# A decode attention and MLP kernel: the tensor engine's wait at a loop's entry, and the layout of the last weight matrix

## The chip, the core and the metric

The kernel runs on one core of one Trainium2 chip. Its engines are TensorE (PE in the profile, its weight loads PEld), VectorE (DVE), ScalarE (ACT), GpSimd (POOL) and SyncE (SP); SP issues nearly all transfers, and its issuing instructions are shown as SPq. The metric is the device time of one execution in microseconds, and the median of several runs is taken. Shorter is better.

## What is computed

One decode step of a transformer block for a batch of 4 tokens, with a cache of 4096 keys and values for each of 32 heads:

```
h  = x + attention(layernorm(x), k_cache, v_cache, wq) @ wo     # D = 640, 32 heads of 128
h2 = h + mish(layernorm(h) @ w1 + b1) @ w2                      # F = 1728
```

Everything is bf16. The key and the value cache are 134 MB each (4 x 32 x 4096 x 128), so the kernel reads 283 MB of memory and does little arithmetic with each number. F = 1728 is 13 chunks of 128 and one of 64.

## The kernel before, in words

**Units and slots.** The batch and the heads are cut into 16 units of 8 heads of one token (`NU` = 16). A unit's keys are one transfer of 128 x 32768 numbers (8.4 MB), and its values another. There are three slots in SBUF, 64 KB on each partition, and keys and values use them in turn: K of unit u and later V of unit u go to slot 2u mod 3 (K of unit 0 to slot 1, and V of unit 0 to slot 0, once wq has been read from there).

**One unit.** VectorE multiplies the keys in place by the broadcast query, in 8 pieces (L585, `times_q`). TensorE sums the products over the head dimension with an identity as weights, 16 matmuls for each quarter (L597, `sums`, into four PSUM banks). VectorE reduces each bank (L572, `reduce`). Then come the maximum (L634, L643, L652), the bias (L665, L674) and the exponentials on ScalarE (L682). TensorE multiplies the *previous* unit's exponentials with its values (L707, `pv`), in program order right behind the current unit's sums, and then closes the unit before that (L739, L741, L760, L767).

**The order of the transfers.** SP issues them in program order, each with the waits it needs: wq, K0, K1, V0, K2, V1, K3, V2, K4 and so on (L333). V of unit u goes into the slot in which K of unit u was, so it waits for that unit's sums. K of unit u+2 waits for the product with the values that lay in its slot, those of unit u-1. The last unit's values come in four parts. Behind them on SP's queue are `wo` (4 transfers), `w1` (5), and `w2` (5; all at L823, in `load`), which go into slots that the last units leave; then the output (L1048).

**Who sets the waits.** The class `Program` records every operation with what it reads and writes, works out the waits (`plan`), and emits each engine's instructions in the recorded order (`emit`). All engines' instructions are straight-line code except TensorE's. Its units 2 to 13 are a loop of 4 turns with 3 units a turn, in which a wait's target is worked out from the turn (`turn * step + base`). A wait inside the loop is kept for an operation only if the engine has not waited for that event before, in the order of the straight program. So that nothing is missed at the first turn, `plan` collects `pe_entry`: for every source, the latest event from before the loop that any operation in the loop depends on. `emit` has TensorE wait for all of these ahead of the loop (L200). Among the sources are other engines' counters and, for unit 2's `pv`, the counter of slot 2, which stands for the transfer of V1. The loop's own wait for that transfer stands in front of `pv`.

**The end.** After the last unit, the 16 outputs are regrouped (L852, L872, L880) and projected with `wo` (L892); a layernorm follows in which the mean is taken out ahead of `w1` and the variance put in afterwards (L929, L937, L971, L983). `h1_pass` (L956) multiplies 14 chunks of columns of `w1` for each of five blocks of 128 rows, so 70 matmuls of 4 columns. The last chunk has only 64 columns; the PSUM rows that it doesn't write are zeroed by VectorE first (L950). The mish function is seven small operations (L852 to L998). `w2_products` (L1024) then does 70 more matmuls, chunk by chunk as parts of `w2` arrive: first the 64 rows left over, then chunks 0 to 5, 6 to 9, 10 and 11, and 12. A residual, a transposition (L1040), a copy (L1047) and the output transfer end the kernel. Chunk c of the hidden vector is rows 128c to 128c+127 of `w2`, one row of 1,280 bytes on a partition.

Of the kernel before, what the change touches and what calls it, by code (L numbers as in the profile page):

```python
# [21 lines left out]
class Program:  # L22
# [53 lines left out]
    def plan(self):  # L76
        by_key = {o.key: o for o in self.ops if o.key is not None}

        def shifted(o, units):
            return by_key.get((*o.key[:-1], o.key[-1] + units)) if o.key else None  # L80


        known = {e: {} for e in self.ENGINES}
        for o in self.ops:
            k = known[o.eng]
            o.waits = []
            for src, d in o.deps.items():
# [12 lines left out]
        before, rest = [], None  # L100
        in_order = [o for o in self.ops if o.eng == "PE"]
        at = [i for i, o in enumerate(in_order) if self.in_loop(o)]
        assert at == list(range(at[0], at[0] + len(body) * turns))
        for t in range(turns):
            for p, b in enumerate(body):
                o = in_order[at[0] + t * len(body) + p]
                assert o is shifted(b, (t - 2) * self.turn), (o.key, b.key)
        self.pe_before = in_order[: at[0]]
        self.pe_after = in_order[at[0] + len(body) * turns :]
        body_waits = [[d for d in b.waits] for b in body]  # L110
        for b in body:
            for d in b.waits:
                assert d.key is not None and d.key[-1] >= self.first + self.turn, (b.key, d.key)


        loop_units = range(self.first, self.last + 1)
        for o in self.ops:
            for d in o.waits:
                d.signal = True
        for o in self.ops:  # L120
            if o.signal and o.key and o.key[-1] in loop_units:
                for u in range(self.first, self.last + 1):
                    same = by_key.get((*o.key[:-1], u))
# [24 lines left out]

        self.body_waits = []
        for b, waits in zip(body, body_waits):  # L150
            out = []
            for d in waits:
                src = d.sem or d.eng
                e = shifted(d, self.turn)
                step = e.count - d.count
                assert step > 0
                for t in range(turns):
                    f = shifted(d, (t - 2) * self.turn)
                    if f is not None and f.key[-1] >= self.first:
# [50 lines left out]
def kernel(  # L210
# [64 lines left out]
    S_BANK, TR, QQ, OB, OT = [("bank", i) for i in range(4)], *[("bank", i) for i in range(4, 8)]  # L275
# [4 lines left out]
    ident = const([128, 128], BF16, "ident")  # L280
# [205 lines left out]
        "DVE", lambda: nc.vector.tensor_copy(out=j_m[:, :], in_=j_f[:, :]), r=["j_f"], w=["j_m"]  # L486
    )

    def f_chunk(rows, c):
        if c < C2:  # L490
            return rows[:, c * 128 : (c + 1) * 128], 128
        return rows[:, FM:F], FREM


    qT_ps = qq_bank[:, 0 : N * H].rearrange("p (b h) -> p b h", b=N)
# [16 lines left out]

    def b1_turned():
        for c in range(FC):
            cols, fw = f_chunk(b1_row, c)
            ins = nc.tensor.matmul(  # L516
                b_ps[0:fw, c : c + 1], lhsT=cols, rhs=ident[0:1, 0:1], start=True, stop=True
            )
        return ins

    def b1_copy():
        nc.vector.tensor_copy(out=b1T[:, 0:C2], in_=b_ps[:, 0:C2])  # L522
        return nc.vector.tensor_copy(out=b1T[0:FREM, C2:FC], in_=b_ps[0:FREM, C2:FC])
# [323 lines left out]
    def do(eng, emit, r=(), w=()):  # L847

        return P.add(eng, emit, r=r, w=w, after=[last_pv])
# [100 lines left out]
    do("DVE", lambda: nc.vector.memset(h1_ps[FREM:128, FC - 1, :], 0.0), (), [QQ])  # L950
    std, rstd = scratch(N), scratch(N)

    def h1_pass(dc):
        for c in (0, C2, *range(1, C2)):
            lhsT, fw = f_chunk(w1_sb[:, dc, :], c)
            ins = nc.tensor.matmul(  # L956
                h1_ps[0:fw, c, :],
                lhsT=lhsT,
                rhs=h2T[:, dc, :],
                start=(dc == 0 and c == 0),  # L960
                stop=(dc == DC - 1 and c == C2 - 1),
            )
        return ins

# [53 lines left out]

    def w2_products(blocks):
        for c in blocks:  # L1020
            rows = 128 if c < C2 else FREM
            w2 = w2_sb[:, c, :] if c < C2 else w2r_sb
            for dc in range(DC):
                ins = nc.tensor.matmul(  # L1024
                    y2T[:, dc, :],
                    lhsT=w2[:, dc * 128 : (dc + 1) * 128],
                    rhs=act_t[0:rows, c, :],
                    start=(c == C2 and dc == 0),
                    stop=(c == C2 - 1 and dc == DC - 1),
                )  # L1030
        return ins

    for name, blocks in ((C2, [C2]), *((k0, range(k0, k1)) for k0, k1 in zip(W2P, W2P[1:]))):
        do("PE", lambda blocks=blocks: w2_products(blocks), [("w2", name), "act"], [S_BANK[1]])
# [48 lines left out]
```

## Time and profile before

| | |
|---|---|
| time, median of 3 runs | 672.83 us (672.2 to 672.95) |
| the profiled execution's own time | 673.69 us |
| its span in the profile | 671.8 us |
| busy: PE, PEld, DVE, ACT, POOL | 380.5, 174.8, 353.2, 88.0, 1.3 us |
| read from memory | 283.35 MB, 422 GB/s over the span |

The span is the time from the first to the last event of the profile; 1.89 us of the execution lie outside it. A row of the waits names the waiting engine with its output and line, what released it, the total of the waits in us, their number and the longest. A row of a timeline has the start and the duration in us, the engine, the line, the operation, output and inputs with their shapes, the number of instructions merged, and in brackets the idle time before it and what ended it. A row of the chain has start, duration, engine or transfer. A row of a windows table has the stretch, its length, the busy time and number of instructions of PE, PEld, DVE, ACT and POOL, TensorE's granted clock, the busy share of the 16 DMA engines and the GB/s that they moved; a transfer packet counts in the window in which it starts. A row of the groups has busy time in us, mean ns of one, and the idle time before.

### The profile page before, as it was taken

How to read it: one execution, taken by the hardware profiler on the slowest of the kernel's cores; microseconds unless marked ns; L12 is line 12 of the kernel's file. 1: busy time of each engine (PE TensorE's matmuls, PEld its weight loads, DVE VectorE, ACT ScalarE, POOL GpSimd, SP SyncE). 2: the span in 40 equal slices, each digit the busy share in tenths (PEclk: the TensorE clock that was granted, in tenths of full speed). 3: DMA queues.
4: the chain of work that ended last, by engine and by line, in shares of the span. 5: the costliest groups of instructions: out<-in, count | busy, mean ns of one | idle time of the engine just before them, and what ended most of it. 6: DMA issues, size and time to landing. Idle time of an engine off the chain costs nothing.

```text
span 671.8 us, 6600 instructions
## 1 busy us (share of the span) xinstructions
PE 380.5 (57%) x2793; PEld 174.8 (26%) x2793; DVE 353.2 (53%) x314; ACT 88.0 (13%) x314; POOL 1.3 (0%) x10
## 2 busy tenths in 40 slices
PE   0366732887282856738184664818375481837764
PEld 0222310333031322213032321303132230313344
DVE  2078840766381836548182754728184563819501
ACT  0102020020202020110202020020202002020211
POOL 0000000000000000000000000000000000000000
PEclk9999975989596796959688796968879695978965
DMA  9999999799999999999999999999999999999997
GB/s 375 438 437 434 433 435 433 328 376 438 433 434 437 437 437 437 433 437 433 421 425 419 437 437 437 433 437 433 433 437 433 437 437 437 434 430 410 412 416 245
DMA packets 8347, 283.62 MB, mean 422 GB/s; under 512 B 835, under 2 KB 2567, under 8 KB 3208
## 3 DMA queue, kind: packets, MB, share of 16 engines
q1 hardware_dynamic: 8318, 283.35, 98.2%
q8 instruction: 12, 0.20, 0.1%
q14 instruction: 7, 0.06, 0.0%
q10 hardware_dynamic: 10, 0.01, 0.0%
HBM read 283.35 MB, written 0.01 MB: 422 GB/s over the span
## 4 chain that ended last, share of the span: by engine, by line
DMA 39%; DVE 28%; PE 20%; another core or an unknown queue 8%; SPq 3%; issue 1%
DMA slot<-in_A_k_cache_dram 33%; DVE slot L585 23%; PE bank L597 14%; PE bank L707 5%; DMA slot<-in_A_v_cache_dram 4%; DVE s_sb L572 3%; SPq L823 3%; DMA slot<-in_B_w_dram 2%; PE bank L665 0%; DVE mx L652 0%; PE bank L643 0%; DVE otn L767 0%; DVE rl L760 0%; PE bank L741 0%
## 5 line engine op out<-in xcount | busy, mean ns | idle before, releaser
L597 PE MATMUL bank<-slot,ident 128*128 128x512 bf16 x1024 | 273.9, 423 | 250.2 <-DVE slot L585 225.6
L585 DVE TENSOR_TENSOR slot<-slot,qb 128x4096 bf16<-128x4096 bf16 x128 | 288.2, 2284 | 145.4 <-DMA slot<-in_A_k_cache_dram 145.4
L597 PEld LDWEIGHTS bank<-slot,ident 128*128 128x128 bf16 x1024 | 101.5, 107 | 408.4 <-DVE slot L585 258.7
L572 DVE TENSOR_REDUCE s_sb<-bank 128x64 f32<-128x512 f32 x64 | 44.0, 688 | 74.5 <-PE bank L597 74.5
L682 ACT ACTIVATE e<-s_sb,nb 128x256 bf16<-128x256 f32 x128 | 63.1, 494 | 46.6 <-DVE nb L674 46.6
L707 PE MATMUL bank<-slot,e 128*32 128x512 bf16 x1024 | 60.7, 391 | 1.5 <-DMA slot<-in_A_v_cache_dram 1.5
L552 ACT CAST qb<-bank 128x128 bf16<-128x128 f32 x16 | 4.2, 265 | 294.5 <-PE bank L543 294.5
L727 ACT COPY o_sb<-bank 128x512 f32<-128x512 f32 x16 | 9.4, 585 | 200.2 <-PE bank L707 200.2
L707 PEld LDWEIGHTS bank<-slot,e 128*32 128x32 bf16 x1024 | 26.5, 99 | 34.1 <-issue 9.0
L652 DVE TENSOR_REDUCE mx<-bank 1x8 f32<-1x128 f32 x16 | 4.5, 279 | 39.9 <-PE bank L643 39.9
L682 ACT ACTIVATION_READ_ACCUMULATOR e<-s_sb,nb 128x1 f32 x128 | 23.9, 187 | 0.0
L741 PE MATMUL bank<-sel,o_sb 128*128 128x8 f32 x128 | 17.4, 263 | 0.0
L741 PEld LDWEIGHTS bank<-sel,o_sb 128*128 128x128 f32 x128 | 16.4, 201 | 0.0
L500 PE MATMUL bank<-xT,slot 128*128 128x4 bf16 x160 | 4.4, 168 | 11.0 <-DMA slot<-in_A_wq_dram 11.0
L665 PE MATMUL bank<-mx,nscale 1*128 1x8 f32 x32 | 6.1, 262 | 5.9 <-DVE mx L652 5.9
L760 DVE RECIPROCAL rl<-bank 128x8 f32<-128x8 f32 x16 | 3.2, 202 | 11.3 <-PE bank L741 11.3
L522 DVE COPY b1T<-bank 128x13 f32<-128x13 f32 x1 | 0.2, 172 | 14.5 <-PE bank L516 14.5
L665 PEld LDWEIGHTS bank<-mx,nscale 1*128 1x128 f32 x32 | 4.7, 183 | 10.6 <-DVE mx L652 10.6
L500 PEld LDWEIGHTS bank<-xT,slot 128*128 128x128 bf16 x160 | 4.3, 104 | 11.1 <-DMA slot<-in_A_wq_dram 11.1
L634 DVE TENSOR_REDUCE pm<-s_sb 128x1 f32<-128x256 f32 x16 | 6.7, 420 | 0.5
L739 PEld LDWEIGHTS bank<-rs,ones_f 128*128 128x128 f32 x32 | 6.1, 198 | 3.2 <-ACT o_sb L727 1.2
L643 PE MATMUL bank<-ident_f,pm 128*1 128x128 f32 x32 | 6.1, 272 | 1.2 <-DVE pm L634 1.2
(73 smaller groups left out, 69.2 us busy)
## 6 DMA issues: line engine op xcount, KB each, us to landing
slot<-in_A_v_cache_dram SPq DMA_DIRECT2D x4, 2048.0 KB, 42.5
slot<-in_A_wq_dram SPq DMA_DIRECT2D x1, 5120.0 KB, 15.5
slot<-in_A_wo_dram SPq DMA_DIRECT2D x4, 1280.0 KB, 33.8
slot<-in_B_w_dram SPq DMA_DIRECT2D x5, 432.0 KB, 29.7
slot<-in_B_w_dram SPq DMA_DIRECT2D x1, 960.0 KB, 20.4
slot<-in_B_w_dram SPq DMA_DIRECT2D x1, 640.0 KB, 19.5
slot<-in_B_w_dram SPq DMA_DIRECT2D x1, 320.0 KB, 10.9
slot<-in_A_k_cache_dram SPq DMA_DIRECT2D x16, 50.2
```

The source lines that it names most:

```text
L500: ins = nc.tensor.matmul(qT_ps[:, :, h], lhsT=wq_sb[:, c, h * Dh : (h + 1) * Dh], rhs=xT[:, c, :], start=(c == 0), stop=(c == DC - 1),)
L572: lambda: nc.vector.tensor_reduce(out=s_sb[:, part * RP : (part + 1) * RP], in_=s_bank[part][:, :].rearrange("p (r w) -> p r w", w=W), axi ...
L585: return nc.vector.tensor_tensor(out=kt, in0=kt, in1=qbs[u % NS][:, k * DQ : (k + 1) * DQ] .unsqueeze(1) .to_broadcast([128, RP, DQ]), op= ...
L597: ins = nc.tensor.matmul(s_bank[part][:, :].rearrange("p (r w) -> p r w", w=W), lhsT=ident[:, :], rhs=kt[:, :, d : d + W], start=(d == 0), ...
L634: lambda: nc.vector.tensor_reduce(out=pm[:, :], in_=s_sb[:, :], axis=AX.X, op=ALU.max),
L643: lambda: nc.tensor.matmul(tr_bank[0:1, 0:128], lhsT=pm[:, :], rhs=ident_f[:, :], start=True, stop=True),
L665: lambda: nc.tensor.matmul(nb_ps, lhsT=nscale[:, :], rhs=mx[:, :], start=True, stop=True),
L682: ins = nc.scalar.activation(out=e2[:, :, h, :], in_=s_sb[:, :].rearrange("p (g r) -> p g r", r=RQ), func=ACT.Exp, bias=nb[:, h : h + 1], ...
L707: ins = nc.tensor.matmul(o_bank[t : t + G * RQ, :], lhsT=e2[:, g, :, :], rhs=vt[:, g * RQ : (g + 1) * RQ, :], start=(g < CT), stop=(g >= N ...
L727: lambda: nc.scalar.copy(out=o_sb[:, :], in_=o_bank[:, :]),
L741: ins = nc.tensor.matmul(o_ps, lhsT=o_sb[:, r * Dh : (r + 1) * Dh], rhs=sel[:, r, :], start=(r == 0), stop=(r == RQ - 1),)
L823: lambda: nc.sync.dma_start(out=out_ap, in_=in_ap),
```

## The change

There are two edits.

The first is one condition in `plan`: an event enters `pe_entry` only if it isn't a transfer's (`d.sem is None`). TensorE's wait for slot 2 at the loop's entry goes; those for DVE, ACT and POOL stay. The wait inside the loop, in front of `pv`, is untouched.

The second changes which hidden column goes with which partition. For the first 12 chunks, chunk 2m takes the even and chunk 2m+1 the odd columns of 256 (`f_rows`), so that one partition holds two neighbouring rows of `w2`, and its transfers move 2,560 contiguous bytes where they moved 1,280. `w1` and `b1` keep their layout in SBUF, and TensorE reads every second column of them as weights. Chunk 12 stays as it was. The last chunk takes the last 128 columns, so that it repeats the last 64 columns of chunk 12 in its upper half; the `w2` rows for these are zeros, written by GpSimd (`w2r`), and the 64 real rows go to partitions 64 to 127. With every chunk 128 wide, three small operations fall away: the zeroing of PSUM (L950) and of `b1T` (L389), and the second of two copies of `b1T` (L523). Both matmul loops now go through the chunks in order.

```diff
-                if d.key is None or d.key[-1] < self.first:
+                if d.sem is None and (d.key is None or d.key[-1] < self.first):
...
+    OVER = 128 - FREM
...
-    P.add("POOL", lambda: nc.gpsimd.memset(b1T[:, :], 0.0), w=["b1T"])
...
+    def f_rows(c):
+        if c < C2 - C2 % 2:
+            f0 = c // 2 * 256 + c % 2
+            return slice(f0, f0 + 255, 2)
+        f0 = c * 128 if c < C2 else F - 128
+        return slice(f0, f0 + 128)
...
-    P.add("DVE", b1_copy, r=[OT], w=["b1T"])
+    P.add("DVE", lambda: nc.vector.tensor_copy(out=b1T[:, :], in_=b_ps), r=[OT], w=["b1T"])
...
-    w2r_sb = wend2[0:FREM, C2 * D : nw2]
-    w2_view = B_w2[0:FM, :].rearrange("(k p) n -> p k n", k=C2)
+    w2r_sb = wend2[:, C2 * D : nw2]
+    C2E = C2 - C2 % 2
+    w2_view = B_w2[0 : C2E * 128, :].rearrange("(m p k) n -> p m (k n)", p=128, k=2)
...
-    load(w2r_sb, B_w2[FM:F, :], i2, C2 * D, nw2, ("w2", C2))
+    P.add("POOL", lambda: nc.gpsimd.memset(w2r_sb, 0.0), w=["w2r"], after=[last_pv])
+    P.add(
+        "SP",
+        lambda: nc.sync.dma_start(out=w2r_sb[OVER:128, :], in_=B_w2[FM:F, :]),
+        w=["w2r"],
+        sem="w2r",
+    )
     for k0, k1 in zip(W2P, W2P[1:]):
-        load(w2_sb[:, k0:k1], w2_view[:, k0:k1], i2, k0 * D, k1 * D, ("w2", k0))
+        if k0 < C2E:
+            to = wend2[:, k0 * D : k1 * D].rearrange("p (m n) -> p m n", n=2 * D)
+            of = w2_view[:, k0 // 2 : k1 // 2]
+        else:
+            to, of = w2_sb[:, k0, :], B_w2[k0 * 128 : k1 * 128, :]
+        load(to, of, i2, k0 * D, k1 * D, ("w2", k0))
...
-    do("DVE", lambda: nc.vector.memset(h1_ps[FREM:128, FC - 1, :], 0.0), (), [QQ])
...
-        for c in (0, C2, *range(1, C2)):
-            lhsT, fw = f_chunk(w1_sb[:, dc, :], c)
+        for c in range(FC):
             ins = nc.tensor.matmul(
-                h1_ps[0:fw, c, :],
-                lhsT=lhsT,
+                h1_ps[:, c, :],
+                lhsT=w1_sb[:, dc, f_rows(c)],
```

More of the change, by code (lines that the diff above doesn't have):

```diff
@@ L487 @@
     )
[L489 to L492, printed above, removed]
+    def f_rows(c):
[4 more added lines that the diff above has]
+        return slice(f0, f0 + 128)
     qT_ps = qq_bank[:, 0 : N * H].rearrange("p (b h) -> p b h", b=N)
@@ L514, in b1_turned @@
         for c in range(FC):
-            cols, fw = f_chunk(b1_row, c)
             ins = nc.tensor.matmul(
-                b_ps[0:fw, c : c + 1], lhsT=cols, rhs=ident[0:1, 0:1], start=True, stop=True
-            )
-        return ins
-    def b1_copy():
-        nc.vector.tensor_copy(out=b1T[:, 0:C2], in_=b_ps[:, 0:C2])
-        return nc.vector.tensor_copy(out=b1T[0:FREM, C2:FC], in_=b_ps[0:FREM, C2:FC])
+                b_ps[:, c : c + 1],
+                lhsT=b1_row[:, f_rows(c)],
+                rhs=ident[0:1, 0:1],
+                start=True,
+                stop=True,
+            )
+        return ins
     P.add("PE", b1_turned, r=["b1", "ident"], w=[OT])
-    P.add("DVE", b1_copy, r=[OT], w=["b1T"])
+    P.add("DVE", lambda: nc.vector.tensor_copy(out=b1T[:, :], in_=b_ps), r=[OT], w=["b1T"])
     def q_broadcast(u, now):
@@ L832 @@
         load(w1_sb[:, c], w1_view[:, c], i1, nwo + c * F, nwo + (c + 1) * F, ("w1", c))
-    load(w2r_sb, B_w2[FM:F, :], i2, C2 * D, nw2, ("w2", C2))
-    for k0, k1 in zip(W2P, W2P[1:]):
-        load(w2_sb[:, k0:k1], w2_view[:, k0:k1], i2, k0 * D, k1 * D, ("w2", k0))
+    P.add(
+        "POOL",
+        lambda: nc.gpsimd.memset(w2r_sb, 0.0),
+        w=["w2r"],
+        after=[last_pv],
+    )
+    P.add(
+        "SP",
+        lambda: nc.sync.dma_start(out=w2r_sb[OVER:128, :], in_=B_w2[FM:F, :]),
+        w=["w2r"],
+        sem="w2r",
+    )
+    for k0, k1 in zip(W2P, W2P[1:]):
+        if k0 < C2E:
+            assert k0 % 2 == k1 % 2 == 0
+            to = wend2[:, k0 * D : k1 * D].rearrange("p (m n) -> p m n", n=2 * D)
[3 more added lines that the diff above has]
+        load(to, of, i2, k0 * D, k1 * D, ("w2", k0))
     at = [nw2]
@@ L949 @@
     h1_ps = qq_bank[:, 0 : FC * N].rearrange("p (c n) -> p c n", c=FC)
-    do("DVE", lambda: nc.vector.memset(h1_ps[FREM:128, FC - 1, :], 0.0), (), [QQ])
     std, rstd = scratch(N), scratch(N)
     def h1_pass(dc):
-        for c in (0, C2, *range(1, C2)):
-            lhsT, fw = f_chunk(w1_sb[:, dc, :], c)
+        for c in range(FC):
             ins = nc.tensor.matmul(
-                h1_ps[0:fw, c, :],
-                lhsT=lhsT,
+                h1_ps[:, c, :],
+                lhsT=w1_sb[:, dc, f_rows(c)],
                 rhs=h2T[:, dc, :],
                 start=(dc == 0 and c == 0),
-                stop=(dc == DC - 1 and c == C2 - 1),
+                stop=(dc == DC - 1 and c == C2),
             )
@@ L1020, in w2_products @@
         for c in blocks:
-            rows = 128 if c < C2 else FREM
             w2 = w2_sb[:, c, :] if c < C2 else w2r_sb
@@ L1026, in w2_products @@
                     lhsT=w2[:, dc * 128 : (dc + 1) * 128],
-                    rhs=act_t[0:rows, c, :],
+                    rhs=act_t[:, c, :],
                     start=(c == C2 and dc == 0),
@@ L1031, in w2_products @@
         return ins
-    for name, blocks in ((C2, [C2]), *((k0, range(k0, k1)) for k0, k1 in zip(W2P, W2P[1:]))):
-        do("PE", lambda blocks=blocks: w2_products(blocks), [("w2", name), "act"], [S_BANK[1]])
+    do("PE", lambda: w2_products([C2]), ["w2r", "act"], [S_BANK[1]])
+    for k0, k1 in zip(W2P, W2P[1:]):
+        do("PE", lambda b=range(k0, k1): w2_products(b), [("w2", k0), "act"], [S_BANK[1]])
     oT = scratch(N * DC, BF16).rearrange("p (n c) -> p n c", n=N)
```

## The prediction

> **What bounds the kernel now.** I read the page's 40 slices first, then the waits, then the timeline of unit 2, then the end. In the page's second part, the row of the GB/s moved:
>
> ```profile
> GB/s 375 438 437 434 433 435 433 328 376 438 433 434 437 437 437 437 433 437 433 421 425 419 437 437 437 433 437 433 433 437 433 437 437 437 434 430 410 412 416 245
> ```
>
> One slice is 671.8/40 = 16.8 us. Nearly all lie at 433 to 437: the transfers set the pace, and no engine does. Three places fall short: the first slice, the last, and slices 8 and 9 (328 and 376, from 117.6 to 151.2 us). The middle one is a hole in the middle of a stream that should have none. The waits name a candidate:
>
> ```profile
> DVE slot L585 <- DMA slot<-in_A_k_cache_dram: 145.4, 14, 14.4
> DVE s_sb L572 <- PE bank L597: 74.5, 32, 19.3
> PE bank L597 <- DMA slot<-in_A_v_cache_dram: 24.6, 1, 24.6
> ```
>
> In general VectorE waits for keys, as it should where transfers bind. But the sums (L597) once waited 24.6 us for *values*, which they don't read. The timeline shows where, and what followed:
>
> ```profile
> 88.60 0.33 SPq L333 DMA_DIRECT2D slot<-in_A_k_cache_dram  x1
> 94.42 6.70 DVE L585 TENSOR_TENSOR slot<-slot,qb 128x4096 bf16<-128x4096 bf16 x3 [4.74 <-DMA slot<-in_A_k_cache_dram]
> 114.08 7.99 PE L597 MATMUL bank<-slot,ident 128*128 128x512 bf16 x24 [24.61 <-DMA slot<-in_A_v_cache_dram]
> 120.38 0.69 DVE L572 TENSOR_REDUCE s_sb<-bank 128x64 f32<-128x512 f32 x1 [19.27 <-PE bank L597]
> 135.62 0.33 SPq L333 DMA_DIRECT2D slot<-in_A_v_cache_dram  x1
> 139.21 0.33 SPq L333 DMA_DIRECT2D slot<-in_A_k_cache_dram  x1
> 178.02 6.70 DVE L585 TENSOR_TENSOR slot<-slot,qb 128x4096 bf16<-128x4096 bf16 x3 [10.23 <-DMA slot<-in_A_k_cache_dram]
> ```
>
> K2 has landed at 94.42, and VectorE multiplies three pieces and stops; TensorE, at the loop's entry, stands until V1 has landed. Unit 2's sums end late, so V2, which needs K2's slot, is issued only at 135.62 and K4 at 139.21. Nothing is queued behind K3 (issued at 88.60). In the windows (packets counted where they start):
>
> ```profile
> 130.00:131.00 1.00, 0.38 (x3) 0.11 (x2) 1.00 (x2) 0.00 (x0) 0.00 (x0) 1.00 0.31 131
> 131.00:132.00 1.00, 1.00 (x6) 0.45 (x5) 1.00 (x2) 0.00 (x0) 0.00 (x0) 1.00 0.00 0
> 135.00:136.00 1.00, 1.00 (x15) 0.36 (x17) 0.42 (x1) 0.00 (x0) 0.00 (x0) 1.00 0.00 0
> 136.00:137.00 1.00, 1.00 (x25) 0.46 (x21) 0.69 (x2) 0.00 (x0) 0.00 (x0) 1.00 2.60 852
> 117.60:151.20 33.60, 27.61 (x172) 12.75 (x171) 24.64 (x20) 5.08 (x19) 0.00 (x0) 0.92 0.83 352
> 150.00:167.00 17.00, 13.93 (x113) 5.91 (x112) 12.31 (x12) 0.59 (x2) 0.00 (x0) 1.00 1.00 433
> ```
>
> K3's last packets start at 130 to 131, V2's first after 136: the transfer engines ran dry. A kernel bound by transfers never gets such time back.
>
> **Part 1: the wait at the entry.** How long is the hole? Three views.
>
> First, by the pace. A unit's keys and values arrive in the time between two units' starts:
>
> ```profile
> 604.38 6.70 DVE L585 TENSOR_TENSOR slot<-slot,qb 128x4096 bf16<-128x4096 bf16 x3 [10.26 <-DMA slot<-in_A_k_cache_dram]
> 201.13 3.57 PE bank L707 x64
> ```
>
> Unit 4 starts at 178.02 and unit 15 at 604.38: (604.38 - 178.02)/11 = 38.76 us a unit. Without a hole K4 would land two units after K2, at 94.42 + 77.52 = 171.94; it landed at 178.02. Lost: 6.1 us.
>
> Second, by bytes: 33.6 us at 352 where 433 is the rule is 33.6 x (1 - 352/433) = 6.3 us, the high end.
>
> Third, by packets: 64 KB at 433/16 GB/s take 2.42 us, so the last ones, started between about 128.6 and 131.0, end at 132.1 on average, and the next start at about 136.8: 4.7 us, the low end. It leaves out that the restart is slow (share 2.60 x 16 for 852 KB, 13 packets, is 3.2 us a packet), so I take 6.1.
>
> Is all of it regained? Unit 2's sums would start at 94.42 and take what unit 4's take, 201.13 - 178.02 = 23.1 us, so V2 is issued at 117.5 and K4 some 3.6 us later (one L707 group): V2 is 11 us ahead of the first of K3's last packets (128.6), and K4 7 us. V1 had landed before 114.08, so the loop's own wait ahead of `pv` at 117.5 finds it there. Late next are the transfers themselves: unit 3 waits for K3 at 94.42 + 38.76 = 133.2, as the later units wait (10.23 and 10.26 us above). Everything behind moves 6.1 us forward.
>
> **Part 2: the end.** These rows are of the old kernel; each comes 6.1 us earlier.
>
> ```profile
> 641.59 2.66 SPq L823
> 644.30 2.64 SPq L823
> 646.98 9.44 SPq L823
> 656.46 10.90 DMA slot<-in_B_w_dram
> 650.00:655.00 5.00, 2.42 (x85) 2.25 (x82) 0.00 (x0) 0.00 (x0) 0.00 (x0) 0.50 0.99 409
> 662.00:664.00 2.00, 0.52 (x13) 0.42 (x13) 1.02 (x5) 0.74 (x3) 0.00 (x0) 0.50 1.07 362
> 658.26 0.26 DVE L852 TENSOR_TENSOR slot<-slot,bank 128x20 bf16<-128x20 f32 x2 [0.68 <-PE bank L937]
> 658.95 1.31 PE L956 MATMUL bank<-slot,slot 128*128 128x4 bf16 x28 [0.73 <-DVE bank L950]
> 660.55 1.97 PE L956 MATMUL bank<-slot,slot 128*128 128x4 bf16 x42
> 664.72 1.16 PE L1024 MATMUL bank<-slot 64*128 64x4 bf16 x35 [2.20 <-DVE slot L998]
> 666.51 0.70 PE L1024 MATMUL bank<-slot 128*128 128x4 bf16 x20 [0.63 <-DMA slot<-in_B_w_dram]
> 667.40 0.70 PE L1024 MATMUL bank<-slot 128*128 128x4 bf16 x15 [0.20 <-DMA slot<-in_B_w_dram]
> ```
>
> The last 15 products wait for a part of `w2` that lands at 656.46 + 10.90 = 667.36. So the end is set by `w2`'s arrival, with 0.63 + 0.20 = 0.83 us of waiting above the products' own time.
>
> *Larger packets.* While `w2` streams (662 to 664), the engines are busy at 1.07 and move 362 GB/s; keys at share 1.00 move 433, `w1` with 3,456 bytes a packet 409. A 1,280-byte packet thus takes 1.07 x 1280 x 16/362 = 60.5 ns and a 64 KB one 2,422 ns: a line of 13.5 ns plus 0.0368 ns a byte, which gives 107.6 ns for 2,560 bytes, against 121.0 for two packets. `w2`'s first 12 chunks are 96 such packets on each engine, so 48 pairs: 48 x 13.4 = 0.65 us. Drawn through `w1`'s row instead (133.8 ns) it is 0.84. Ends: 0 and 0.84; I take 0.65.
>
> The Trainium skill (DMA: Bandwidth & Descriptors, Specifications) gives 512 bytes as the least transfer for line rate. By that rule 1,280-byte packets have it already, this part would bring nothing, and the sum would be 6.1. The measured 362 against 433 at a full busy share speaks against it, and I go by the row.
>
> *Every second column.* 60 of `h1`'s 70 weight loads step over two columns. The old kernel has one strided load, five columns a step, in the first of two L442 groups (4.4 to 5.1 us); the second group (5.1 to 5.6) reads neighbours:
>
> ```profile
> L442 PEld LDWEIGHTS bank<-ident,slot 4*128 4x128 bf16 x5 | 0.3, 125 | 4.5 <-DVE slot L425 4.5
> L442 PEld LDWEIGHTS bank<-ident,slot 4*128 4x128 bf16 x5 | 0.2, 99 | 0.4 <-issue 0.4
> L741 PEld LDWEIGHTS bank<-sel,o_sb 128*128 128x128 f32 x8 | 1.8, 334 | 0.0
> ```
>
> At most 26 ns a load, 60 x 26 = 1.6 us; a step of two lies nearest to a step of one, so I take a quarter, 0.4 us. Against it, `h1` no longer waits for the zeroing behind four VectorE operations: its input is the first of the two at 658.26, done by 658.39, so it starts about 0.4 us earlier. These cancel, and `w2`'s arrival hides the rest on either side up to 0.83 us. Beyond that cover a delay counts in full.
>
> *The zeros on GpSimd and the queue behind them.* The `w2r` transfer now waits for a GpSimd operation, and four `w2` transfers stand behind it on SP.
>
> ```profile
> L367 POOL MEMSET ident<- 128x128 bf16 x1 | 0.2, 204 | 0.5 <-SPq L1050 0.5
> 627.64 3.57 PE bank L707 x64
> ```
>
> It is released when the last `pv` of the loop over units ends, 631.21, and takes five times 0.204, about 1.0 us. SP reaches the transfer only at 641.59, so 9 us cover it; without them each `w2` part would be 1.0 us later.
>
> *Nothing for the rest.* One copy and one zeroing of `b1T` fall away in the first 22 us, where VectorE waits for K0 anyway; the five leftover products use 128 rows instead of 64 (they are among the 35 that take 1.16 us); the chunk order moves no instruction to another engine.
>
> **Sum.** The profiled execution took 673.69 (span 671.8, 1.89 outside): 673.69 - 6.1 - 0.65 = 666.9. It was 0.86 above the median of the runs, so against 672.83 the forecast is 666.1.
>
> **Rivals.**
> - *The end gains nothing* because packets of 1,280 bytes lose nothing by their size (the rule above), or because strided loads eat the gain: 672.83 - 6.1 = 666.7. Against it stands the 362; for it, that the last two packets' landings also hold fixed time. Chance 0.27.
> - *The hole closes only in part.* Unit 2 then runs beside V1's and K3's transfers, and the hole was partly restart: 4.7 us, no gain at the end, 668.1. Chance 0.07. Against it, the later units also run beside transfers, at 433.
> - *The wait only moves.* If V2 were still issued too late, by a stall of unit 2 elsewhere of 13 us or more, the hole would stay and only the end would change: 672.2. Nothing in the rows shows such a stall. Chance 0.03.
> - *Slower:* strided weight loads as slow as the f32 ones (L741: 1.8 us for 8, so 225 ns each, where `h1` has 1.31/28 = 47). That is 60 x 178 = 10.7 us on the path, less 0.4 and 0.83: 672.83 - 6.1 + 9.5 = 676.2. It decides from (6.1 + 0.4 + 0.83)/60 = 122 ns more a load; the step-of-five row says 26 at most. Chance 0.03.
>
> **How the numbers follow.** The forecast has 0.60; its own range is 6.3 + 0.84 = 7.1 to 6.1 + 0.3 = 6.4 below, 665.7 to 666.4, widened by the runs' spread of 0.4 to 665.3 to 666.8. With the first two rivals the range is 664.9 to 668.2, which leaves out the last two and some scatter. A change of 0.2% (1.3 us) is about what a measurement tells from none: faster 0.94, same 0.03 (the third rival), slower 0.03.
>
> **What would show it.** Right: the one L597 wait for values gone; K4's first multiplication at about 172; slices 8 and 9 near 433; V2 issued at about 118; unit 15 at about 598.3; the `w2` windows near 2,560 x 16 x 1.07/107.6 ns = 407 GB/s at a share of 1.07; the last products about 6.7 us earlier. Wrong: a dry stretch elsewhere, L956 groups longer than 3.7 us in sum, or SP standing at `w2r`. If the transfers turn out to have slack that I don't see, the 6.1 us come back as waits of VectorE for keys.

## The result and the profile after

The changed kernel takes 668.09 us (median of 6 runs, 667.80 to 668.28), the old one on the same chip 672.90 (6 runs, 672.20 to 673.37). The ratio is 0.9929, with an interval from 0.9916 to 0.9941: 4.8 us less. The forecast was 666.1 in a range of 664.9 to 668.2, so sign and range held, and the time came out 2.0 us above the forecast, nearly at the range's upper edge. That edge came from a rival (668.1); the forecast's own range, 665.3 to 666.8, missed the time by 1.3 us. The profiled execution took 667.87 us, 666.0 of them its span. Most of this section shows steps that came out as forecast; the last rows show where they did not.

From the page of the changed kernel, the GB/s of the 40 slices (16.65 us each):

```profile
GB/s 378 438 441 434 441 434 425 419 437 442 421 438 433 437 429 433 433 441 421 437 437 433 437 429 429 441 425 425 437 441 437 433 429 437 430 418 427 420 416 241
```

The 328 and 376 of slices 8 and 9 are gone; there stand 419 and 437. Its waits:

```profile
DVE slot L587 <- DMA slot<-in_A_k_cache_dram: 158.7, 15, 14.8
DVE s_sb L574 <- PE bank L599: 55.7, 32, 2.3
```

The sums no longer wait for values. VectorE's longest wait for sums fell from 19.3 to 2.3 us, and its waits for keys rose by 13.3 us: the time is spent waiting for the transfers, as everywhere else. The timeline, units 2, 3, 4 and 15:

```profile
94.34 6.69 DVE L587 TENSOR_TENSOR slot<-slot,qb 128x4096 bf16<-128x4096 bf16 x3 [4.17 <-DMA slot<-in_A_k_cache_dram]
96.69 7.32 PE L599 MATMUL bank<-slot,ident 128*128 128x512 bf16 x24 [6.72 <-DVE slot L587]
117.56 0.33 SPq L335 DMA_DIRECT2D slot<-in_A_v_cache_dram  x1
121.15 0.33 SPq L335 DMA_DIRECT2D slot<-in_A_k_cache_dram  x1
133.06 6.70 DVE L587 TENSOR_TENSOR slot<-slot,qb 128x4096 bf16<-128x4096 bf16 x3 [10.84 <-DMA slot<-in_A_k_cache_dram]
171.81 6.70 DVE L587 TENSOR_TENSOR slot<-slot,qb 128x4096 bf16<-128x4096 bf16 x3 [11.44 <-DMA slot<-in_A_k_cache_dram]
598.04 6.70 DVE L587 TENSOR_TENSOR slot<-slot,qb 128x4096 bf16<-128x4096 bf16 x3 [11.31 <-DMA slot<-in_A_k_cache_dram]
```

Unit 2's sums start 2.35 us behind VectorE's first piece. V2 is issued at 117.56 (135.62 before), K4 at 121.15 (139.21), and unit 15 starts at 598.04 (604.38): 6.34 us earlier. The windows, the first over the old hole, the last three over `w2`:

```profile
117.60:151.20 33.60, 17.83 (x129) 8.21 (x122) 18.89 (x16) 5.08 (x19) 0.00 (x0) 0.80 1.00 434
136.00:137.00 1.00, 1.00 (x4) 0.30 (x2) 1.00 (x1) 0.00 (x0) 0.00 (x0) 0.50 0.91 393
656.00:658.00 2.00, 0.54 (x14) 0.45 (x14) 0.65 (x3) 0.67 (x3) 0.00 (x0) 0.50 1.03 376
658.00:660.00 2.00, 0.84 (x32) 0.87 (x33) 0.91 (x4) 0.00 (x0) 0.00 (x0) 0.50 0.76 289
660.00:661.00 1.00, 0.48 (x18) 0.40 (x16) 0.00 (x0) 0.00 (x0) 0.00 (x0) 0.50 0.34 123
```

There is no dry stretch at 136. But at the end the share falls to 0.76 and 0.34 before the last part lands: most transfer engines are done, and some are late (the records further down put 3.4 us between the first and the last). The end's timeline, then its piece of the chain, then two groups:

```profile
650.64 1.23 PE L912 MATMUL bank<-slot,slot 128*128 128x4 bf16 x40 [1.88 <-DMA slot<-in_A_wo_dram]
653.30 0.89 PE L974 MATMUL bank<-slot,slot 128*128 128x4 bf16 x28 [0.36 <-DVE slot L872]
654.48 0.51 PE L974 MATMUL bank<-slot,slot 128*128 128x4 bf16 x14
655.28 0.53 PE L974 MATMUL bank<-slot,slot 128*128 128x4 bf16 x14 [0.29 <-DMA slot<-in_B_w_dram]
656.42 0.54 PE L974 MATMUL bank<-slot,slot 128*128 128x4 bf16 x14 [0.62 <-DMA slot<-in_B_w_dram]
```

```profile
648.41 13.12 DMA slot<-in_B_w_dram
661.53 0.05 issue
661.58 0.72 PE bank L1041 x15
```

```profile
L974 PEld LDWEIGHTS bank<-slot,slot 128*128 128x128 bf16 x70 | 2.4, 107 | 1.5 <-DMA slot<-in_B_w_dram 1.1 <-issue 0.4
L838 POOL MEMSET slot<- 128x640 bf16 x1 | 0.6, 631 | 623.3 <-PE bank L709 623.3
```

The last parts of `w2` still set the end: the last but one lands at 661.53, and the last 15 products start at 661.58 (the last part, chunk 12's, lands while they run), 5.8 us earlier than before, though unit 15 started 6.34 us earlier. (Of the two loops over chunks, only `h1_pass` now goes through them in order; `w2_products` still takes the last chunk first, as before.) From unit 15's start to the last `wo` group it is 650.64 - 598.04 = 52.60 us. To compare, that group in the old kernel:

```profile
655.92 1.23 PE L892 MATMUL bank<-slot,slot 128*128 128x4 bf16 x40 [1.89 <-DMA slot<-in_A_wo_dram]
```

There the stretch takes 655.92 - 604.38 = 51.54 us. So 1.06 us are given back in a stretch that the change doesn't touch. That, and the 2.0 us against the forecast, is what the experiments ask about. Theory A: the hole was worth less in the ordinary run than in the profiled one. Theory B: the new layout costs over 1 us. Theory C: without the hole something is given back behind it, with either layout.

### The profile page after: what moved, and what is told of

Read it like the earlier page. It is cut to its first block, busy times and chain, and to the rows that moved or that the text cites. A ratio compares the mean times of both kernels' runs of the same rounds, so it can differ in the third digit from the quotient of the medians.

```text
span 666.0 us, 6596 instructions
## 1 busy us (share of the span) xinstructions
PE 378.1 (57%) x2793; PEld 173.2 (26%) x2793; DVE 353.2 (53%) x312; ACT 88.0 (13%) x314; POOL 1.9 (0%) x10
## 4 chain that ended last, share of the span: by engine, by line
DVE 31%; DMA 29%; PE 24%; another core or an unknown queue 14%; SPq 1%; issue 1%
DMA slot<-in_A_k_cache_dram 27%; DVE slot L587 26%; PE bank L599 15%; PE bank L709 7%; DVE s_sb L574 4%; DMA slot<-in_B_w_dram 2%; SPq L826 1%; PE bank L667 1%; DVE mx L654 0%; PE bank L645 0%; DVE otn L769 0%; DVE slot L872 0%; DVE rl L762 0%; PE bank L743 0%
## 5 line engine op out<-in xcount | busy, mean ns | idle before, releaser
L762 DVE RECIPROCAL rl<-bank 128x8 f32<-128x8 f32 x16 | 3.2, 202 | 11.8 <-PE bank L743 11.8
```

## The experiments

The old kernel ran beside each group; its medians there were 673.23 (15 runs; e1 to e4), 672.98 (9; e5 to e8) and 672.92 (13; e9 to e11).

### One edit alone: e1 and e2

e1 is the old kernel with the first edit only, e2 the new kernel without it, e3 the new kernel once more.

```diff
 e1, in the old kernel:
-                if d.key is None or d.key[-1] < self.first:
+                if d.sem is None and (d.key is None or d.key[-1] < self.first):
 e2, in the new kernel:
-                if d.sem is None and (d.key is None or d.key[-1] < self.first):
+                if d.key is None or d.key[-1] < self.first:
 e3: the new kernel, nothing changed
```

> The kernel before with the one condition in `plan` alone: TensorE no longer waits for V1 at the loop's entry, and the layout of w2 is the old one. The changed kernel's median fell by 4.8 us where 6.75 were forecast, and its trace shows unit 15 starting 6.3 us earlier but `wo`'s last group only 5.3 us earlier. Theory A (the hole is worth 4.8 to 5.3 us in an ordinary execution, because the profiled execution of before was 0.8 us slower than its median, and the layout brings some tenths): 667.7 to 668.3 us. Theory B (the entry is worth the 6.2 us that unit 15 shows, and the new layout costs over 1 us): 666.5 to 666.9 us. Theory C (what is regained in the loop is partly given back between unit 15 and `wo`, with either layout): 668.3 to 668.8 us, with 52.6 us from unit 15's first multiplication to the last `wo` group where before had 51.5.

> The changed kernel with the old condition in `plan`: TensorE waits for V1 at the loop's entry again, and the layout of w2, w1's columns and the zeros on GpSimd are the new ones. Theory A: 672.2 to 672.6 us (0.3 to 0.65 us less than before). Theory B: 673.9 to 674.5 us. Theory C: 672.2 to 672.6 us, with 51.5 us from unit 15's first multiplication to the last `wo` group. By all three, V2 is issued at 135 to 136 us and the hole is back.

> The changed kernel as it is, a second trace and more times, on the same chip as the two halves: 667.8 to 668.3 us. If the stretch from unit 15's first multiplication to the last `wo` group is 52.6 us again, the 1.06 us there belong to the kernel; if it is 51.5, they are the scatter of one execution.

Measured: e1 668.36 (668.17 to 669.05; ratio 0.9933, 0.9919 to 0.9946), e2 672.37 (671.68 to 673.21; 0.9988, 0.9979 to 0.9997), e3 668.25 (667.78 to 668.30; 0.9928, 0.9914 to 0.9941). The timeline of e1:

```profile
118.22 0.33 SPq L333 DMA_DIRECT2D slot<-in_A_v_cache_dram  x1
171.92 6.70 DVE L585 TENSOR_TENSOR slot<-slot,qb 128x4096 bf16<-128x4096 bf16 x3 [10.83 <-DMA slot<-in_A_k_cache_dram]
598.00 6.70 DVE L585 TENSOR_TENSOR slot<-slot,qb 128x4096 bf16<-128x4096 bf16 x3 [10.59 <-DMA slot<-in_A_k_cache_dram]
650.61 1.23 PE L892 MATMUL bank<-slot,slot 128*128 128x4 bf16 x40 [1.92 <-DMA slot<-in_A_wo_dram]
```

The same of e2:

```profile
113.99 7.17 PE L599 MATMUL bank<-slot,ident 128*128 128x512 bf16 x24 [24.08 <-DMA slot<-in_A_v_cache_dram]
134.71 0.33 SPq L335 DMA_DIRECT2D slot<-in_A_v_cache_dram  x1
603.43 6.69 DVE L587 TENSOR_TENSOR slot<-slot,qb 128x4096 bf16<-128x4096 bf16 x3 [10.78 <-DMA slot<-in_A_k_cache_dram]
654.86 1.23 PE L912 MATMUL bank<-slot,slot 128*128 128x4 bf16 x40 [1.89 <-DMA slot<-in_A_wo_dram]
```

The first edit brings 4.9 us with the old layout and 4.1 with the new one, the second 0.9 where the hole is left and 0.1 (668.36 to 668.25) where it is closed; the last of these is below what the runs tell apart. B falls: the layout alone doesn't cost. C is borne out: with the old layout and no hole, e1's stretch is 650.61 - 598.00 = 52.61 us, as in the new kernel (52.60, and 52.63 in e3, so the 1.06 us are not the scatter of one execution); with the new layout and the hole, e2's is 654.86 - 603.43 = 51.43, as in the old one. The give-back goes with the hole. The times alone would not have told C from A, which is open beside it (see e11). From the last `wo` group to the end of the span it is 15.88 us before, 15.99 in e1, 15.44 in e2 and 15.36 in the new kernel: there the layout is worth 0.4 to 0.6.

### Larger packets still: e4

Four rows of `w2` to a partition, `h1` by every fourth column, parts of `w2` cut at 0, 4, 8, 12.

```diff
-    W2P = (0, 6, 10, 12, C2)
+    W2P = (0, 4, 8, 12, C2)
...
-        if c < C2 - C2 % 2:
-            f0 = c // 2 * 256 + c % 2
-            return slice(f0, f0 + 255, 2)
+        if c < C2 - C2 % 4:
+            f0 = c // 4 * 512 + c % 4
+            return slice(f0, f0 + 509, 4)
```

> The changed kernel with four rows of w2 to a partition instead of two: packets of 5,120 bytes for the first 12 chunks, `h1` by every fourth column of w1, and the parts of w2 cut at chunks 4, 8 and 12. If packet size sets the pace of w2 (two 1,280-byte packets take 121 ns, one of 2,560 bytes about 108 to 113), a packet of 5,120 takes about 202 ns and another 24 x 14 ns = 0.3 us are gained over the changed kernel: 667.6 to 667.9 us. If size no longer matters there: 668.1 us. If weight loads with a step of four columns are slower, the L974 passes take more than 0.55 us each.

Measured: 667.81 (667.58 to 668.04; ratio 0.9923, 0.9909 to 0.9936). It has the lowest median of all, 0.3 to 0.4 below the new kernel's, with overlapping spreads, so the 0.3 us expected of larger packets are not told apart from scatter. Two of its `h1` groups (the first answers to 0.89 us in the new kernel):

```profile
653.42 1.04 PE L974 MATMUL bank<-slot,slot 128*128 128x4 bf16 x28 [0.36 <-DVE slot L872]
654.75 1.27 PE L974 MATMUL bank<-slot,slot 128*128 128x4 bf16 x28
```

A step of four columns is 5 ns a matmul slower than a step of two in the first group (1.04/28 = 37 ns against 0.89/28 = 32). The cover of `w2`'s arrival takes it: the last products of e4 still wait 0.81 us for `w2`.

### How late may unit 2 be? e5 and e6

The hole is opened again by other means. In e5, 61 matmuls of 512 columns, whose results nothing reads, stand on TensorE in front of unit 2's sums; in e6 107 of them.

```diff
+    def stall():
+        for _ in range(61):          # 107 in e6
+            ins = nc.tensor.matmul(
+                oT_bank[:, :].rearrange("p (a n) -> p a n", a=4),
+                lhsT=ident[:, :],
+                rhs=ident[:, :].unsqueeze(1).to_broadcast([128, 4, 128]),
+                start=True, stop=True)
+        return ins
...
+        if u == 2:
+            P.add("PE", stall, r=["ident"], w=[OT])
```

> The changed kernel with 61 matmuls of 512 columns on TensorE ahead of the loop, on constants, whose result nothing reads. They run from about 89.5 to about 104.7 us, so unit 2's sums start some 8 us late: a delay at the same place as the wait that was removed, of half its length. If only a dry transfer queue costs time, V2 is issued at about 125, still ahead of K3's last packets (128.6 to 131), and the time stays at 668.2 us within 0.5. If each us of delay at the loop's entry costs its share (17.4 us of delay cost 4.9), the time is 670.5 us.

> The same with 107 such matmuls, to about 114.7 us, so that unit 2's sums start some 18 us late, as late as in the kernel before, with no wait for a transfer. If the dry queue is what costs, V2 is issued at 135 to 136, the two slices from 117.6 to 151.2 us move 350 to 370 GB/s, and the time is 672.4 us within 0.7 (that of the layout alone). If the wait for a transfer itself is what costs, 668.2 us.

Measured: e5 668.16 (667.87 to 668.32; ratio 0.9925, 0.9910 to 0.9941), e6 669.41 (667.88 to 670.33; 0.9942, 0.9926 to 0.9958). The timeline of e5:

```profile
89.25 13.34 PE L787 MATMUL bank<-ident 128*128 128x512 bf16 x61
102.42 5.34 PE L599 MATMUL bank<-slot,ident 128*128 128x512 bf16 x24
121.32 0.33 SPq L335 DMA_DIRECT2D slot<-in_A_v_cache_dram  x1
172.07 6.69 DVE L587 TENSOR_TENSOR slot<-slot,qb 128x4096 bf16<-128x4096 bf16 x3 [10.23 <-DMA slot<-in_A_k_cache_dram]
```

The same of e6:

```profile
89.44 23.27 PE L787 MATMUL bank<-ident 128*128 128x512 bf16 x107
112.55 1.67 PE L599 MATMUL bank<-slot,ident 128*128 128x512 bf16 x7
131.44 0.33 SPq L335 DMA_DIRECT2D slot<-in_A_v_cache_dram  x1
173.90 6.70 DVE L587 TENSOR_TENSOR slot<-slot,qb 128x4096 bf16<-128x4096 bf16 x3 [11.38 <-DMA slot<-in_A_k_cache_dram]
```

In e5 unit 2's sums start 5.7 us late (102.42 against 96.69; 8 were meant), and K4's first multiplication comes at 172.07, among the 171.76 to 172.08 of the other kernels without a hole. In e6 they start 15.9 us late (18 were meant), V2 is issued at 131.44 and not at 135 to 136, no packet starts from 131 to 132, and K4's first multiplication comes 2.1 us late. So e6 makes only a small hole, and the 672.4 us expected of a whole one were not reached; what it has to show is that the time rises although no sum waits for a transfer. Where V2 was late, K4 came 42.4 us behind V2's issue: 178.02 - 135.62 = 42.40 before, 42.36 in e2, 42.46 in e6. With 171.8 as K4's earliest time, V2 may be issued up to about 129.4, so the new kernel has 11.8 us of cover (11 forecast). In these two runs it is the dry queue that costs, and not the wait as such.

### What is given back, and why: e7 to e10

For each transfer the trace holds one completion for each of the 16 transfer engines. The Trainium skill (DMA: Bandwidth & Descriptors, Why a DMA increments its semaphore by 16 and not by 1) says the same: up to 16 engines finish independently, and the semaphore counts them; the records here agree, with engines up to 3.8 us apart. The first column is the time from the first engine's completion of V13 to the first engine's completion of the last `wo` transfer; the others are how far the last engine is behind the first at the landing named, all in us:

```
            first engine:  last engine behind the first, at
            last wo        V13   K15   V14   V15, part 3   last wo   last w2
before      70.72          1.84  2.07  2.21  2.20          2.22      2.15
e2          70.72          2.01  2.14  2.18  2.18          2.18      2.14
after       70.72          2.02  2.19  3.00  3.39          3.40      3.37
e1          70.81          2.06  2.09  2.99  3.28          3.23      3.07
e9          70.72          2.98  2.99  2.99  3.05          3.33      3.29
```

The first engine takes the same 70.7 to 70.8 us with and without the hole. The last one falls behind it by 0.8 to 0.9 us between K15 and V14 and by another 0.3 to 0.4 later, and it does so only in the kernels without the hole (in e9, read below, the first step comes earlier). Since the last engine sets when a transfer has landed, that is the give-back. The hole itself shows in the same records: V2's landing has a spread of 0.73 us in the old kernel, where V1's had 1.93. An empty queue brings the engines together again. In e6, with its small hole, V2's spread is 1.18 us, V14's 2.62, and the stretch 52.05 us, in between.

What holds one engine up? The page of the new kernel has, among the queues, two that carry instructions (packets, MB, share):

```profile
q8 instruction: 12, 0.20, 0.1%
q14 instruction: 7, 0.06, 0.0%
```

A packet of each lies between K15 and V14, at about 613 us (queue 14, 8 KB) and 616 us (queue 8, 16 KB) of the records. If it is the cause, moving it moves the step. A few instructions at the start, whose results nothing reads, shift an engine's later fetches: e7 and e8 put 64 and 128 matmuls of one column on TensorE, e9 64 zeroings of one element on VectorE, e10 60 copies of one column on ScalarE.

```diff
+    def pad_code():                  # e7; range(128) in e8
+        for _ in range(64):
+            ins = nc.tensor.matmul(oT_bank[0:1, 0:1], lhsT=ident[0:1, 0:1],
+                                   rhs=ident[0:1, 0:1], start=True, stop=True)
+        return ins
+    P.add("PE", pad_code, r=["ident"], w=[OT])
...
+    def pad_dve():                   # e9
+        for k in range(64):
+            ins = nc.vector.memset(s_sb[0:1, k : k + 1], 0.0)
+        return ins
+    P.add("DVE", pad_dve, w=[("s_sb", 0)])
...
+    def pad_act():                   # e10
+        for k in range(60):
+            ins = nc.scalar.copy(out=o_sb[0:N, k : k + 1], in_=eps_t[0:N, :])
+        return ins
+    P.add("ACT", pad_act, r=["eps"], w=["o_sb"])
```

> The changed kernel with 64 one-column matmuls on TensorE at the start, where it waits for wq: no work on the path, but TensorE's code is 128 instructions longer, so that its later instruction fetches (16 KB packets on queue 8, one transfer engine each, about 1.1 us) come half a fetch earlier in the work. In the four kernels without the hole, one of the 16 transfer engines falls 0.85 us behind the others between K15's and V14's landing, beside such a fetch, and unit 15's first multiplication to the last wo group takes 52.6 us; in the two with the hole, 51.5. If a fetch that hits an engine which is already among the last is what gives back the 1.1 us, that stretch changes by 0.3 us or more either way, and the time with it: 667.2 to 668.8 us, not 668.2. If the stretch has another cause, it stays at 52.6 within 0.15 and the time at 668.2.

> The same with 128 such matmuls, 256 instructions, which is one whole fetch: the later fetches come at the same points of the work, but each with the next block of the code. If the engine that a fetch goes to follows from the block, the engine that falls behind is another and the stretch from unit 15's first multiplication to the last wo group differs from 52.6 us; if it follows from anything that goes with the place in the work, it stays at 52.6 within 0.15. Time 667.2 to 668.8 us by the first, 668.2 by the second.

> The changed kernel with 64 one-element memsets on VectorE at the start, where it waits for the first keys: no work on the path, but VectorE's code is 64 instructions longer. Padding TensorE's code did not move the stretch from unit 15's first multiplication to the last wo group (52.61 both times), though its own fetches moved. The one instruction packet that lies between K15's and V14's landing in every kernel is an 8 KB one on queue 14 (at about 613 us of the trace records). If that one is VectorE's and it is what puts one transfer engine 0.9 us further back, it comes about half a fetch (some 3 units) earlier, a K interval of about 39.5 us appears there, and the stretch falls to 51.6 to 52.0 us, with the whole time still 667.8 to 668.4. If the packet is not VectorE's, or not the cause, the stretch stays at 52.6 within 0.15.

> The same with 60 one-element copies on ScalarE at the start, before it has q to convert: ScalarE's code is 60 instructions longer. If the 8 KB packet on queue 14 is ScalarE's and it is the cause, the stretch from unit 15's first multiplication to the last wo group falls to 51.6 to 52.0 us; if not, it stays at 52.6 within 0.15. Whole time 667.8 to 668.4 us either way.

Measured: e7 668.07 (ratio 0.9925, 0.9912 to 0.9939), e8 667.95 (0.9923, 0.9910 to 0.9937), e9 667.98 (0.9926, 0.9909 to 0.9943), e10 667.93 (0.9926, 0.9909 to 0.9942). The stretch from unit 15 to the last `wo` group is 52.61 us in e7 and e8, 52.51 in e10, and 51.72 in e9. The timeline of e9 shows where its part went:

```profile
481.87 6.70 DVE L594 TENSOR_TENSOR slot<-slot,qb 128x4096 bf16<-128x4096 bf16 x3 [10.15 <-DMA slot<-in_A_k_cache_dram]
521.55 6.70 DVE L594 TENSOR_TENSOR slot<-slot,qb 128x4096 bf16<-128x4096 bf16 x3 [11.69 <-DMA slot<-in_A_k_cache_dram]
560.27 6.70 DVE L594 TENSOR_TENSOR slot<-slot,qb 128x4096 bf16<-128x4096 bf16 x3 [10.09 <-DMA slot<-in_A_k_cache_dram]
598.99 6.70 DVE L594 TENSOR_TENSOR slot<-slot,qb 128x4096 bf16<-128x4096 bf16 x3 [10.68 <-DMA slot<-in_A_k_cache_dram]
650.71 1.23 PE L919 MATMUL bank<-slot,slot 128*128 128x4 bf16 x40 [2.16 <-DMA slot<-in_A_wo_dram]
```

From unit 12 to unit 13 it is 39.68 us, where the neighbours have 38.72. In the records, e9's spread steps from 2.02 to 2.98 us between the landings at 492.9 and 513.3 (by the records' clock, which reads 11.1 us more than the timeline), and an 8 KB instruction packet on queue 14 has moved from about 613 to 497.3 on the same clock. So the padding of VectorE moved packet and step together. TensorE's padding moved TensorE's own fetches (in e7 from 616 to 595 and 632) and not the step, and ScalarE's moved ScalarE's packet (600 to 487) and not the step. The cause of the first step is VectorE's fetch of instructions, which sets back one of the 16 transfer engines. The total stays the same wherever it falls.

The same records show why the old kernel is spared. They don't name the engine of a completion, but between two fetches the 16 distances behind the first engine stay nearly the same, and at a fetch of VectorE one of them goes and another comes that is 0.9 to 1.0 us larger. There are three such fetches, at about 110, 380 and 613 us of the records (earlier in e9). The distance that goes and the one that comes, in us:

```
            first fetch     largest distance     second fetch    third fetch
                            when V2 has landed
before      0.35 -> 1.31    0.73                 0.27 -> 1.24    1.24 -> 2.21
e2          0.14 -> 1.10    0.81                 0.23 -> 1.21    1.20 -> 2.18
after       0.07 -> 1.04    1.84                 1.04 -> 2.02    2.03 -> 3.00
e1          0.01 -> 0.99    1.92                 0.98 -> 1.99    1.99 -> 2.99
```

This reads as one engine that is set back by each fetch. In the old kernel the hole wipes out the first setback, and the engine ends at 2.21, where the next one stands at 2.06. Without the hole all three add up to 3.00, where the next one stands at 2.19. The second step is of the same kind, by a 16 KB fetch of TensorE, which moves one distance by 1.5 to 1.6 us: in the new kernel the fetch at 638.0 takes one from 1.84 to 3.39 (part 3 of V15), in e7, whose padding has put a fetch at 631.7, one goes from 1.67 to 3.19 at part 1, and in the old kernel the fetch at 643.6 takes one from 0.21 to 1.74, which is not the last. Why a packet of VectorE that itself takes 0.3 us sets an engine back by 0.97 is not shown.

### The old kernel again: e11

```diff
 the old kernel, nothing changed
```

> The kernel before as it is, a second trace. The profiled execution of before was 0.8 us above the median of its runs. If that excess lies in the hole, by the clock that TensorE was granted when it left the wait (24 matmuls in 7.99 us, against 7.17 in the trace of the layout alone), then this trace, with a time near 673.0, has V2 issued nearer 134.8 than 135.6 and K4's first multiplication at V2's issue plus 42.4 us, some 177.2. If the excess lies elsewhere, V2 is issued at 135.6 again and K4 lands at 178.0, with the time at 673.0. Unit 15's first multiplication to the last wo group: 51.5 us.

Measured: 673.53 (672.26 to 673.94; ratio 1.0002, 0.9992 to 1.0011), profiled 673.55. The profiled execution again had a long hole: V2 issued at 135.76, K4's first multiplication at 178.19, against 134.71 and 177.07 in e2, whose profiled time (672.08) lay 0.3 below its median. The windows behind the long wait, of the old kernel, of e11 and of e2, in this order; the third number from the end is TensorE's granted clock:

```profile
118.00:122.00 4.00, 4.00 (x18) 1.75 (x16) 1.62 (x2) 0.00 (x0) 0.00 (x0) 0.82 1.06 459
```

```profile
118.00:122.00 4.00, 4.00 (x16) 1.67 (x15) 1.49 (x2) 0.00 (x0) 0.00 (x0) 0.78 1.10 475
```

```profile
118.00:122.00 4.00, 4.00 (x25) 2.44 (x23) 2.53 (x2) 0.00 (x0) 0.00 (x0) 1.00 1.06 459
```

After the wait the clock stands at 0.50; by the trace's clock records it rises to 1.00 at 119.45, 119.77 and 117.71, which is 5.4, 5.7 and 3.7 us after the wait's end. The 24 sums took 7.99, 8.16 and 7.17 us, and V2's issue followed. So the hole is up to about 1 us longer or shorter by the clock. This run did not settle whether the ordinary execution of the old kernel has the shorter hole, since its own profile lay again at the long end. The scatter of the times points to the hole: from the lowest to the highest run it is 1.1 to 1.7 us in every group with the whole hole, 2.45 in e6, and 0.2 to 0.9 in every group without a hole. So theory A is likely for the 0.8 us by which the old kernel's first profile lay above its median, but it is not shown.

## Why the prediction was right, and what it missed

**The wait at the entry: right, to some tenths.** The hole closed whole: unit 15 came 6.34 us earlier where 6.1 was forecast, V2 at 117.56 (117.5), unit 3 at 133.06 (133.2), K4 at 171.81 (171.94). Of the three views, the one by bytes (6.3) came nearest. The rival by which the hole closes only in part gave 668.1, which is the time that came out, but for a reason that is not the one found: nothing of the hole was left. That the time lies in the stated range is owed to this rival's bound, and so to luck.

**"Everything behind moves 6.1 us forward": the step that failed.** The units did; the stretch behind unit 15 took 52.60 us instead of 51.54. The step took the landing times for those of one stream, and they are those of the slowest of 16. The hole had cost its length to the leading engines, but it had also wiped out the first of three setbacks that VectorE's fetches give one engine. Without it they add up to 3.00 us where they made 2.21, and a fetch of TensorE adds to the last engine's distance once more. So the prediction's sentence that a kernel bound by transfers never gets such time back is too strong: about 1 us of the hole was made good further down the stream. The forecast had no term for that: 1.06 us.

**Larger packets: right in kind, a little too high.** In the window from 656 to 658 the share is 1.03 at 376 GB/s, so 365 at a full share, against 362/1.07 = 338 before and 407/1.07 = 380 forecast. A packet of 2,560 bytes takes 2560 x 16/365 = 112 ns rather than 107.6. By the Trainium skill (DMA: Bandwidth & Descriptors, Specifications), 1,280 bytes already have line rate; 338, 365 and the keys' 434 at share 1.00 disagree. The end is shorter by 15.88 - 15.36 = 0.52 us, 0.65 forecast.

**Every second column: nothing, where 0.4 was taken.** A load took 107 ns, and 108 for neighbouring columns before. The groups became faster, for another reason that the forecast missed. The old kernel's `h1` by forms:

```profile
L956 PE MATMUL bank<-slot,slot 128*128 128x4 bf16 x65 | 2.9, 169 | 0.7 <-DVE bank L950 0.7
L956 PEld LDWEIGHTS bank<-slot,slot 128*128 128x128 bf16 x65 | 2.6, 108 | 0.9 <-issue 0.8
L956 PE MATMUL bank<-slot,slot 128*64 128x4 bf16 x5 | 1.1, 214 | 0.0
L956 PEld LDWEIGHTS bank<-slot,slot 128*64 128x64 bf16 x5 | 0.6, 128 | 0.1
```

The five chunks of 64 columns cost 128 ns a load and 214 a matmul. From start to start, two matmuls on chunks of 128 columns lie 25 to 29 ns apart in the trace, but it is mostly 94 to 96 ns to a chunk of 64 and 144 to 148 from it to the next, with 47 to 49 behind that. Without them 28 matmuls take 0.89 us instead of 1.31. `h1` starts 0.36 us behind VectorE instead of 0.73, as forecast. It gained nothing at the end, since `h1` now waits for `w1` (0.29 and 0.62 us) and the last products for `w2`.

**The zeros on GpSimd: hidden, as forecast.** They took 0.63 us (1.0 estimated), from 625.56, and SP issues the transfer behind them at 636.29, over 9 us after their end.

**The sum.** From profiled to profiled execution the forecast was 673.69 - 6.75 = 666.94, and 667.87 came: 0.93 too low. The terms: -0.24 for the hole, +1.06 given back, +0.13 at the end, -0.02 outside the span. The other 1.1 us of the miss came with turning this into a median: the forecast took off 0.86 because the profiled execution of before lay that far above its median, while the new kernel's lay 0.22 below its own. That excess can't be taken off once more if it lay in the hole, which the change removes. The clock rows and the scatter above fit that; they don't prove it.

## What to carry to other kernels

In a kernel bound by transfers, look for the slice whose rate dips, and from there for the wait that holds back the *issue* of the next transfer; a wait of 24.6 us cost 6 us here, and a delay of 5.7 us cost nothing, because only the time with an empty queue counts. A gain ahead of a long stream of transfers need not arrive whole at its end: a landing is the slowest of 16 engines, and here each fetch of instructions set one of them back, and they met again only where the queue ran dry. And before an offset between the profiled execution and the median is subtracted, ask whether it lies in the very stretch that the change removes.

## What the hardware showed that I had not expected

- The 16 transfer engines keep their distances over hundreds of us: the spread of the landings stays at 1.84 to 1.89 us through 18 landings of the new kernel. A dry queue brings it from 1.93 to 0.73 in the old one.
- A fetch of 8 KB of instructions for VectorE sets one transfer engine back by 0.9 to 1.0 us, one of 16 KB for TensorE by 1.5 to 1.6, and that engine doesn't catch up while the queue is full.
- After the queue ran dry, the two transfers of 8.4 MB that follow need 42.4 us from the issue of the first to the use of the second, where the pace is 38.7 us: a restart costs 3.7 us. With the 2.5 us from K3's landing (133.10) to V2's issue (135.62) this makes the 6.2 us that the hole cost.
- Weights with a step of two columns load as fast as neighbouring ones (107 against 108 ns), while 64 columns load slower than 128 (128 ns against 108).
